# Tokens kept in natural order, values in chunks of 128 tokens, and a re-ordered start of the first batch

## The chip, the cores and the metric

The kernel runs on one core of one Trainium2 chip. The metric is the device time of one execution in microseconds (us). The median of three runs of the kernel before is 842.7 us (839.12 to 846.02).

## What is computed

Three blocks follow one another. All numbers are float32.

```python
# q, k, v: (4 batches, 8 heads, 576 tokens, 64);  M = 32 landmarks of 18 neighbouring tokens each
q_lm = q.reshape(B, H, 32, 18, D).mean(axis=3);  k_lm likewise
A  = softmax(q    @ k_lm.T / 8)      # 576 x 32
Bm = softmax(q_lm @ k_lm.T / 8)      # 32 x 32
C  = softmax(q_lm @ k.T / 8)         # 32 x 576
Z  = Bm.T / (norm_1(Bm) * norm_inf(Bm) + 1e-6)
for _ in range(6): Z = 2 * Z - Z @ Bm @ Z
x = (A @ Z @ C @ v)                  # heads side by side: 2304 tokens x 512
x = silu(x @ w_in) @ w_out           # first MLP: 512 -> 2048 -> 512
xn = x / rms(x) * rms_g              # second MLP: 512 -> 1536 -> 512
out = (silu(xn @ w_gate) * (xn @ w_val)) @ w_out2
```

## The kernel before

**Stages.** A head (0 to about 34 us) does the attention of batch 0 for both groups `g` of four heads, in an order written out by hand in the strings of `HEAD`. Each name there is a step (`qs00` is step `qs0` of group 0, `sc11` is `sc1` of group 1), and `go` records the steps one after the other. `Queue` makes every step's instructions follow the last one on the same engine, so the string is the order on each engine. Then the first MLP runs over batches 0 to 3, two halves of 288 tokens each (`moe1_h`, then `moe1_out`, LAG 3 steps later). The attention of the next batch is woven into it by the generators `attention` (g = 0, 1), whose order among the other work a scheduler sets by its own estimate of when operands are ready. From about 408 us the second MLP runs in 36 equal steps (`moe2_step`) on three blocks of 768 tokens.

**The attention's result is not formed.** The factor Z C v is multiplied into `w_in` first: `lt` holds minus (Z C v), `wprime` multiplies it with a quarter `nb_` of `w_in` into `W'` (`pw` in PSUM), and splits W' into a high and a low float32r part (`wp`: an ACT cast, then a DVE subtraction). `moe1_h` multiplies W' with the split softmax of A (`at`). So the first matmul `h` of a batch needs `lt`, `wp` and `at`.

**Token order.** The host lays q and k out as [64 x 2 partitions, 2, R = 18, M = 32]: the tokens of one landmark are 32 words apart. A sum over a landmark's 18 tokens is stored as row R of the same tile; in the head `summed` does it in one strided DVE reduction, or in five POOL additions where `BY_POOL` says so (three of the eight sums), and `landmarks` in six DVE additions for batches 1 to 3. The exponentials of C are written to `ec` in [32, 18] order (a stride of 18 words), so that v can come as [96 partitions, 4 heads, 6 tokens x 64]; `ct` then takes six transposes and `pu` 24 small matmuls per group. Since all later stages keep the landmark order, `split_x` reorders tokens when it splits x, and `store_out` writes pairs of rows 18 rows apart.

**Weights.** `w_in`, `w_out` and others come as 8-byte numbers and are converted on the chip by two ACT instructions (steps `Wa`, `oa`, lines 182, 183) and two DVE instructions (`Wd`, `We`, `od`, `oe`, lines 187, 189). In batch 0 `LOAD_AT` and `CONV_AT` say after which of the first steps a tile is loaded and converted, `WP_AT` when a further quarter of W' is made. `z1`, `y12` are spare matmuls (`spares`) which write nothing that is used.

Of the kernel before, what the change touches and what calls it, by code (L numbers as in the profile page):

```python
# [45 lines left out]
BY_POOL = {("q", 0, 0): False, ("q", 0, 1): True, ("q", 1, 0): False, ("q", 1, 1): True, ("k", 0, 0): False, ("k", 0, 1): False, ("k", 1, 0): False, ("k", 1, 1): True}  # L46
HEAD = [
    """y12 tab qs00 qs10 ks10 ks00 sc10 qs11 qs01 sc00 ks01 ks11 mx10 sc01 mx20 nb00 T00 ec10 mxl0 nb10 mA00 bbx0 T10
    sc11 su00 ec20 rc10 rr10 mA10 wa00 bbs0 cta0 su10 bbT0 mx11 ctb0 z1 bbd0 mx21 p10 ccb0 cca0 nb01 mxl1 nb11 T01
    z2 ec11 pua0 cr0 rc00 ic10 rr00 ec21 ic20 pub0 rt00 mA01 bbx1 rtu0 cta1 wa10 su01 rc11 rr11 rc01 pe00 z1 bbs1  # L50
    bbT1 bbd1 cp00 cca1 ctb1 rr01 wd00 p11 ccb1 wd10 pua1 xA00 xA01 pub1 cr1 xA10 ic11 pe10 sA01 z1 wa01 ic21 rtu1
    rt01 cp10 sA00 wa11 pe01 z1 wd01 pe20 z1 ms00 we00 cp01 oa13 pe11 cp20 z1 wd11 pe30 z1 we10 cp11 oa12 pe21 z1
    cp30 we01 pe40 z1 we11 cp21 pe31 z1 cp40 ms01 mr00 mr01 cp31 mu00 T11 pe50 pe41 mA11 z1 mu01 cp50 sb00 cp41 su11
    pe51 sb01 ac00 od12 pl0 cp51 ac01 pl1 al00 lt0 xA11 al01 lt1 sA10 tab2 pw z3 ms10 oe12 mr10 sA11 wc00 mu10 wc01
    ms11 wl00 wc10 wl01 wc11 wl10 oa14 wl11 sb10 od13""",
    """ac10 mr11 oe13 Wa00 mu11 al10 sb11""",
    """od14 ac11""",
    """al11 oa15 oe14 Wd00""",
    """od15 Wa10 We00 oe15 Wa11 Wd10""",
    """Wd11 Wa01 We10 We11""",  # L60
    """Wd01 We01""",
# [22 lines left out]
def nystrom_moe_kernel(ctx: ExitStack, tc: tile.TileContext, q, k, v, w_in, w_out, w_gate, w_val, w_out2, rms_g, out):  # L84
# [85 lines left out]

    def to_f32(c, raw, act=1024, dve=1024, out=None):
# [51 lines left out]
    def load_win(n, g):  # L223
# [6 lines left out]
        win_t[g, quarter(n)] = t  # L230

# [39 lines left out]

# [20 lines left out]
    def head(g):  # L292
# [32 lines left out]
        for x, y in (("q", q), ("k", k)):  # L325
            src[x] = big(f"{x}T", [P, 2, R + 1, M])
            SP.dma_start(out=src[x][:, :, 0:R], in_=y[0, g])
        yield
        vn = xp.tile([96, 4, 6 * D], F32, tag="x", name=f"vn_{n}")
        SP.dma_start(out=vn, in_=v[0, g])  # L330

        def summed(x, i):
            t = src[x][:, int(i)]
            if BY_POOL[x, g, int(i)]:
                d = sm("lms", [P, 2, 4, M]).rearrange("p i r l -> p (i r) l")
                QG.tensor_tensor(d, t[:, 0:8], t[:, 8:16], op=ALU.add)
# [34 lines left out]
        def _():  # L371
            QV.tensor_reduce(u["mx"][:, 1:2], c[2][:, :NC2], axis=AX.X, op=ALU.max)
# [1142 lines left out]
```

## Time and profile before

| | |
|---|---|
| median of 3 runs | 842.7 us |
| the profiled execution | 841.08 us |
| its span in the trace | 839.2 us |
| PE busy | 821.5 us, 98% |
| DVE busy | 534.6 us, 64% |
| ACT busy | 448.1 us, 53% |
| POOL busy | 20.8 us, 2% |

The trace covers the span; 1.9 us of the execution lie around it. A busy PE is not PE at its peak: the busy time counts from a matmul's start to its modelled end. PE is TensorE's matmuls, DVE VectorE, ACT ScalarE, POOL GpSimd, SP the engine that issues most DMAs. What matters is where PE has no work and what it waits for there.

### The profile page before, as it was taken

The numbers are of one execution on the slowest core, as the hardware profiler recorded it, in microseconds if no ns is written. First come the engines' busy times: TensorE is split into PE (matmuls) and PEld (weight loads), VectorE is DVE, ScalarE is ACT, GpSimd is POOL, SyncE is SP. The second block draws the span as 40 slices with busy tenths as digits, with TensorE's granted clock in tenths as the row PEclk, the third lists the DMA queues.
The fourth block names the chain that finished last, engine by engine and source line by source line (L and its number), as shares of the span: only waits on it lengthen the run. The fifth ranks groups of instructions, "written<-read, shape, count | busy, mean of one in ns | idle before, by whom it ended". The sixth has DMA issues, their size and how long they took to land.

```text
span 839.2 us, 15513 instructions
## 1 busy us (share of the span) xinstructions
PE 821.5 (98%) x5956; PEld 735.3 (88%) x5956; DVE 534.6 (64%) x1196; ACT 448.1 (53%) x927; POOL 20.8 (2%) x60
## 2 busy tenths in 40 slices
PE   7999999999999999999999999999999999999997
PEld 5667677988888989999999999999999999999996
DVE  6989868785679767769735389643558533333323
ACT  4886755775657767675734457433345323233222
POOL 5100000000000000000000000000000000000001
PEclk9999999999999999999999999999999999999999
DMA  9989557358886579988975458668565558655542
GB/s 304 393 286 326 196 170 258 121 176 299 285 289 193 167 263 354 351 304 295 329 309 189 174 197 286 242 228 295 210 226 209 183 184 289 226 222 189 181 197 76
DMA packets 72426, 202.87 MB, mean 242 GB/s; under 512 B 6592, under 2 KB 34240, under 8 KB 68384
## 3 DMA queue, kind: packets, MB, share of 16 engines
q1 hardware_dynamic: 72032, 201.09, 67.3%
q8 instruction: 47, 0.77, 0.4%
q0 software_dynamic: 240, 0.66, 0.3%
q14 instruction: 27, 0.22, 0.1%
q10 hardware_dynamic: 80, 0.13, 0.0%
HBM read 149.29 MB, written 52.56 MB: 241 GB/s over the span
## 4 chain that ended last, share of the span: by engine, by line
PE 87%; ACT 5%; DVE 4%; DMA 2%; issue 1%; POOL 1%; SPq 0%; POOLq 0%; ACTq 0%; DVEq 0%
PE ga L1180 18%; PE o L1254 18%; PE a L1031 18%; PE h L1011 10%; PE gc L1180 9%; PE gb L1180 5%; PE a L1028 3%; PE pw L843 2%; PE pe L270 1%; DMA r_g<-in_moe_w_gate_dram 1%; DMA qT<-in_q_dram 1%; PE pu L781 0%; PE pq L264 0%; POOL lms L284 0%; DVE hl L165 0%
## 5 line engine op out<-in xcount | busy, mean ns | idle before, releaser
L1031 PE MATMUL a<-hl,wo 128*128 128x288 f32 x1296 | 195.7, 299 | 2.2 <-ACT ex L1059 1.2
L1031 PEld LDWEIGHTS a<-hl,wo 128*128 128x128 f32 x1296 | 177.9, 188 | 8.5 <-issue 2.5
L1254 PE MATMUL o<-oc,u 128*128 128x512 f32 x648 | 178.9, 394 | 0.0
L1180 PE MATMUL ga<-x,w 128*128 128x384 f32 x840 | 171.1, 338 | 0.0
L1180 PEld LDWEIGHTS ga<-x,w 128*128 128x128 f32 x840 | 151.3, 188 | 12.4 <-ACT a L198 0.3
L1254 PEld LDWEIGHTS o<-oc,u 128*128 128x128 f32 x648 | 119.4, 188 | 13.6 <-DVE u L165 0.3
L1011 PE MATMUL h<-at,wp 128*128 128x288 f32 x768 | 129.3, 303 | 1.6 <-ACT wp L846 1.4
L1011 PEld LDWEIGHTS h<-at,wp 128*128 128x128 f32 x768 | 109.6, 188 | 18.2 <-issue 5.0
L198 DVE TENSOR_TENSOR v<-u,gc 128x384 f32<-128x384 f32 x72 | 39.8, 552 | 122.1 <-PE gc L1180 121.6
L1018 ACT ACTIVATE s<-h 128x288 f32<-128x288 f32 x108 | 44.1, 412 | 77.1 <-PE h L1011 75.3
L1180 PE MATMUL gc<-x,w 128*128 128x384 f32 x420 | 84.8, 336 | 0.0
L1180 PEld LDWEIGHTS gc<-x,w 128*128 128x128 f32 x420 | 75.0, 188 | 2.9
L198 ACT COPY u<-ga 128x384 f32<-128x384 f32 x72 | 34.5, 479 | 72.1 <-PE ga L1180 71.8
L198 DVE TENSOR_TENSOR u<-z,v 128x384 f32<-128x384 f32 x72 | 40.1, 557 | 46.7 <-ACT z L198 45.8
L164 ACT CAST u<-u 128x384 fp32r<-128x384 f32 x72 | 37.0, 513 | 61.4 <-DVE u L198 61.0
L165 DVE TENSOR_TENSOR hl<-s,hl 128x288 fp32r<-128x288 f32 x108 | 49.0, 453 | 20.4 <-ACT hl L164 19.7
L165 DVE TENSOR_TENSOR u<-u,u 128x384 fp32r<-128x384 f32 x72 | 40.1, 556 | 26.2 <-ACT u L164 25.9
L198 ACT ACTIVATE z<-ga 128x384 f32<-128x384 f32 x36 | 17.7, 492 | 68.5 <-PE ga L1180 68.3
L164 ACT CAST hl<-s 128x288 fp32r<-128x288 f32 x108 | 46.6, 433 | 2.7
L1028 PE MATMUL a<-s,wor 128*128 128x288 f32 x160 | 43.3, 409 | 0.0
L1180 PE MATMUL gb<-x,w 128*128 128x384 f32 x210 | 42.4, 336 | 0.0
L1180 PEld LDWEIGHTS gb<-x,w 128*128 128x128 f32 x210 | 37.0, 188 | 0.2
(230 smaller groups left out, 950.5 us busy)
## 6 DMA issues: line engine op xcount, KB each, us to landing
w<-w7d SPq DMA_DIRECT2D x31, 1792.0 KB, 7.4
oc<-wod SPq DMA_DIRECT2D x32, 512.0 KB, 7.8
win<-wind SPq DMA_DIRECT2D x20, 512.0 KB, 4.8
w2d<-c SPq DMA_DIRECT2D x36, 256.0 KB, 3.3
fw<-w2d SPq DMA_DIRECT2D x12, 768.0 KB, 6.4
winr<-in_moe_w_in_dram SPq DMA_DIRECT2D x8, 1024.0 KB, 10.2
wor<-in_moe_w_out_dram SPq DMA_DIRECT2D x16, 512.0 KB, 11.2
w7d<-w7p SPq DMA_DIRECT2D x16, 512.0 KB, 5.2
```

The lines of the kernel that those rows point to most:

```text
L164: x = ACT.copy(dst[:, 0], src) if hi is ACT else hi.tensor_copy(dst[:, 0], src)
L165: return x, lo.tensor_tensor(dst[:, 1], src, dst[:, 0].bitcast(F32), op=ALU.subtract)
L198: self.last = getattr(self.eng, name)(*args, **kw)
L270: eng.matmul(out[o], x[o], y[o], **kw)
L843: x = PE.matmul(pw[g][32 * i:32 * i + 32], lts[b][hr, i], win_t[i // 2, nb_][hr, i % 2], start=True, stop=True)
L1011: h_mm[0] = PE.matmul(ph, w[:, x, fo:fo + P], a[:, y, tk], start=i == 0, stop=i == 5)
L1018: ACT.activation(s, ph, AF.Silu)
L1028: PE.matmul(acc[d], w[:, y], hl, start=start, stop=stop)
L1031: PE.matmul(acc[d], w[:, x, y], hl[:, z], start=start and i == 0, stop=stop and i == 2)
L1180: mm[0] = PE.matmul(acc, w7[:, x, o, kk], xs[:, y, kk], start=start and n == 0, stop=stop and n == 5, skip_group_check=True)
L1254: PE.matmul(oacc[n], hls[j][:, x, t * P:(t + 1) * P], w[:, y], start=f == 0 and i == 0, stop=f == NF2 - 1 and i == 2)
```

## The change

Tokens keep their natural order everywhere: q and k are laid out as [128, 2, 576], the sums stand behind them in columns S to S + M, `ec` is [128, 576] and written contiguously. v comes as four chunks of 128 tokens and one of 64, in two DMAs per group (`values`); a group then takes five transposes (`turn`) and 20 small matmuls (`weigh`). `landmarks` is one DVE reduction per tensor, only one of the head's eight sums is still on POOL. `split_x` and `store_out` need no reordering. The first W' is made in three parts (`pwa`, `pwb`, `pwc`: 128, 128 and 256 columns) and the spare matmuls `z` are 128x128 with `ident` instead of 128x512 with `mean_w`. The strings of `HEAD` and the tables `WP_AT`, `LOAD_AT`, `CONV_AT` are new, and later quarters of W' in batch 0 have a raised priority for their matmuls and an explicit predecessor.

```diff
-BY_POOL = {("q", 0, 0): False, ("q", 0, 1): True, ("q", 1, 0): False, ("q", 1, 1): True, ("k", 0, 0): False, ("k", 0, 1): False, ("k", 1, 0): False, ("k", 1, 1): True}
+BY_POOL = {("q", 0, 0): False, ("q", 0, 1): False, ("q", 1, 0): False, ("q", 1, 1): True, ("k", 0, 0): False, ("k", 0, 1): False, ("k", 1, 0): False, ("k", 1, 1): False}
...
-    pe51 sb01 ac00 od12 pl0 cp51 ac01 pl1 al00 lt0 xA11 al01 lt1 sA10 tab2 pw z3 ms10 oe12 mr10 sA11 wc00 mu10 wc01
-    ms11 wl00 wc10 wl01 wc11 wl10 oa14 wl11 sb10 od13""",
+    T10 lt0 lt1 al01 Wa10 T11 pwa pwb mA11 pwc z1 mA10 wca0 su11 wca1 wla0 wcb0 wla1 wcb1 su10 wlb0 wcc0 wlb1 wcc1
+    wlc0 xA11 wlc1 xA10 sA11 tab2 ms11 sA10 mr11 ms10 od12 mu11""",
...
-WP_AT = (7, 9, 12)
+WP_AT = (7, 10, 14)
...
+    def values(b, g):
+        t = xp.tile([P, 5, 4, D], F32, tag="x", name=f"vn_{b}_{g}")
+        n = P * 16 * D
+        SP.dma_start(out=t[:, 0:4].rearrange("p c h d -> p (c h d)"), in_=v[b, g, 0:n].rearrange("(p f) -> p f", p=P))
+        SP.dma_start(out=t[0:VC[4], 4].rearrange("p h d -> p (h d)"), in_=v[b, g, n:].rearrange("(p f) -> p f", p=VC[4]))
+        return t
...
-                QV.tensor_reduce(t[:, R], t[:, 0:R].rearrange("p r l -> p l r"), axis=AX.X, op=ALU.add)
+                QV.tensor_reduce(t[:, S:], r, axis=AX.X, op=ALU.add)
...
-            QA.activation(keys()[:, R1:], c[2][:, :NC2].rearrange("p (r l) -> p r l", l=M), AF.Exp, ...)
+            QA.activation(keys()[:, C1:], c[2][:, :C2], AF.Exp, ...)
...
+        for x, lo, hi in (("a", 0, 128), ("b", 128, 256), ("c", 256, 512)):
+            y = slice(lo, hi)
+            step["pw" + x] = lambda y=y: mm(y)
...
-                VE.tensor_tensor(d, t[:, :, 0:4], t[:, :, 4:8], op=ALU.add)
-            for x in (8, 12):
-                VE.tensor_tensor(d, d, t[:, :, x:x + 4], op=ALU.add)
-            VE.tensor_tensor(d[:, :, 0:2], d[:, :, 0:2], d[:, :, 2:4], op=ALU.add)
-            VE.tensor_tensor(d[:, :, 0:2], d[:, :, 0:2], t[:, :, 16:R], op=ALU.add)
-            VE.tensor_tensor(t[:, :, R], d[:, :, 0], d[:, :, 1], op=ALU.add)
+                VE.tensor_reduce(t[:, :, S:], t[:, :, 0:S].rearrange("p i (l r) -> p i l r", r=R), axis=AX.X, op=ALU.add)
...
-            ACT.copy(blocked(t[:, 0, i]), by_landmark(c[:, i]))
+            ACT.copy(t[:, 0, i], c[:, i])
...
-            (SP, POOL, ACT)[h and last].dma_start(out=out[b * S:(b + 1) * S, :].rearrange("(l r) d -> l r d", r=R)[:, r:r + 2], in_=e[64 * h:64 * h + 64])
+            (SP, POOL, ACT)[h and last].dma_start(out=out[row + 64 * h:row + 64 * h + 64], in_=e[y])
```

The first place is DVE in the head, where the second group's chain of six iterations is set up. `cr_1`, `ic_1`, `rc_1` and `rt_0_125` belong to group 1, `pe_..` are the iterations of Z, `winr_0` and `win_0` the conversion of the first `w_in` quarter. Before:

```order
L284 COPY rt_1_124<-pe_0_0_352 128x96
L284 RECIPROCAL rc_1_233<-rc_1_233 128x1
L284 SCALAR_TENSOR_TENSOR winr_0_135<-winr_0_135 128x512 x2
L284 TENSOR_REDUCE cr_1_408<-p_0_1_373 128x2
L284 TENSOR_SCALAR ic_1_409<-cr_1_408 128x1
L284 TENSOR_REDUCE ms_1_232<-sa_1_228 128x9
L284 RECIPROCAL ic_1_409<-ic_1_409 128x1
L284 TENSOR_SCALAR rt_0_125<-pu_1_381,rc_1_233,ic_1_409 128x64
L284 SCALAR_TENSOR_TENSOR rt_0_125<-p_0_1_373,ic_1_409,id_98 128x32
```

and now:

```order
L309 TENSOR_REDUCE cr_1_364<-p_0_1_344 128x2
L309 TENSOR_SCALAR ic_1_365<-cr_1_364 128x1
L309 COPY rt_1_124<-pe_0_0_354 128x96
L309 RECIPROCAL ic_1_365<-ic_1_365 128x1
L309 TENSOR_REDUCE ms_1_227<-sa_1_223 128x9
L309 SCALAR_TENSOR_TENSOR rt_0_125<-p_0_1_344,ic_1_365,id_98 128x32
L309 TENSOR_SCALAR rt_0_125<-pu_1_370,rc_1_228,ic_1_365 128x64
L309 SCALAR_TENSOR_TENSOR winr_0_135<-winr_0_135 128x512
```

The weight conversion stood ahead of group 1's `rt`; now it stands behind it.

The second place is PE in batch 0, where the second quarter of W' is made (`pw_0`, eight rows in both, of which the last stands here) and first used (`h_0_0`). `a_..` are the products with `w_out`, named by half, part and output block. Before:

```order
L843 MATMUL pw_0_1_805<-win_1_155,lt_572 32x512
L1028 MATMUL a_1_0_0_788<-s_1_13_732,wor_147 128x288
L1011 MATMUL h_0_0_818<-at_0_552,wp_0_803 128x288 x2
L1028 MATMUL a_1_0_1_789<-s_1_13_732,wor_147 128x288
L1028 MATMUL a_1_0_2_790<-s_1_13_732,wor_147 128x288
L1011 MATMUL h_0_0_818<-at_0_552,wp_0_803 128x288
```

and now:

```order
L849 MATMUL pw_0_1_797<-win_1_160,lt_550 32x512
L1034 MATMUL a_0_0_0_690<-s_0_15_687,wor_153 128x288
L1034 MATMUL a_0_0_1_691<-s_0_15_687,wor_153 128x288
L1034 MATMUL a_0_0_2_692<-s_0_15_687,wor_153 128x288
L1034 MATMUL a_0_0_3_693<-s_0_15_687,wor_153 128x288
L1034 MATMUL a_1_0_0_780<-s_1_12_707,wor_147 128x288
L1034 MATMUL a_1_0_1_781<-s_1_12_707,wor_147 128x288
L1034 MATMUL a_1_0_2_782<-s_1_12_707,wor_147 128x288
L1034 MATMUL a_1_0_3_783<-s_1_12_707,wor_147 128x288
L1017 MATMUL h_0_0_810<-at_0_529,wp_0_795 128x288 x3
```

One `a` row stood between the last `pw_0` and the first `h_0_0`; now there are eight.

The third place is DVE at the same time: the low part of that quarter (`wp_0`) and the landmark sum of batch 1 (`qT_0` under L200). Before:

```order
L187 SCALAR_TENSOR_TENSOR wor_623<-wor_623 128x512
L189 SCALAR_TENSOR_TENSOR wor_623<-wos_798,wor_623 128x512
L187 SCALAR_TENSOR_TENSOR winr_2_619<-winr_2_619 128x1024
L847 TENSOR_TENSOR wp_0_803<-pw_0_0_804,wp_0_803 128x512
L847 TENSOR_TENSOR wp_0_803<-pw_0_1_805,wp_0_803 128x512
L189 SCALAR_TENSOR_TENSOR win_2_742<-win_2_742,winr_2_619 128x1024
```

and now:

```order
L309 SCALAR_TENSOR_TENSOR wor_153<-wos_710,wor_153 128x512
L200 TENSOR_REDUCE qT_0_819<-qT_0_819 128x2x32
L189 SCALAR_TENSOR_TENSOR winr_2_615<-winr_2_615 128x1024
L853 TENSOR_TENSOR wp_0_795<-pw_0_0_796,wp_0_795 128x512
L853 TENSOR_TENSOR wp_0_795<-pw_0_1_797,wp_0_795 128x512
```

The sum over q of batch 1, which needs a load, has come ahead of the low part of W'.

## Rows read from the trace of the kernel before

**Rows 1.** The page, part 1: engine, busy us (share of span), instructions.

```profile
PE 821.5 (98%) x5956; PEld 735.3 (88%) x5956; DVE 534.6 (64%) x1196; ACT 448.1 (53%) x927; POOL 20.8 (2%) x60
```

**Rows 2.** By stretch: length; busy PE, PEld, DVE, ACT, POOL; clock; DMA share, GB/s.

```profile
0.00:33.83 33.83, 27.35 (x444) 17.45 (x444) 25.89 (x77) 18.91 (x48) 14.54 (x48) 1.00 0.95 347
33.83:60.00 26.17, 24.81 (x151) 18.81 (x151) 22.18 (x35) 23.39 (x45) 0.99 (x1) 1.00 0.85 308
60.00:280.00 220.00, 215.92 (x2051) 183.20 (x2051) 173.70 (x452) 149.57 (x315) 2.41 (x6) 1.00 0.67 228
...
420.00:820.00 400.00, 399.78 (x2076) 371.12 (x2075) 199.25 (x384) 157.74 (x311) 0.00 (x0) 1.00 0.60 222
```

**Rows 3.** Order of time, PE, head: start, length, instruction, [idle before <-releaser].

```profile
13.82 0.43 PE L284 MATMUL pq<-qT,kT 64*32 64x288 f32 x1 [0.99 <-POOL kT L284]
...
22.96 0.37 PE L284 MATMUL pe<-rt 32*32 32x96 f32 x8 [0.32 <-DVE rt L284]
...
23.79 0.37 PE L284 MATMUL pe<-rt 32*32 32x96 f32 x8
...
33.83 3.49 PE L1011 MATMUL h<-at,wp 128*128 128x288 f32 x24
```

**Rows 4.** Order of time, DVE, head.

```profile
10.43 1.12 DVE L284 TENSOR_REDUCE kT<-kT 128x32 f32<-128x576 f32 x1 [0.30 <-DMA kT<-in_k_dram]
```

**Rows 5.** Order of time, POOL, head.

```profile
13.52 0.25 POOL L284 TENSOR_TENSOR kT<-lms 128x32 f32<-128x32 f32 x1
```

**Rows 6.** Groups by line and form: busy us, mean ns, idle before.

```profile
L284 DVE TENSOR_REDUCE kT<-kT 128x32 f32<-128x576 f32 x3 | 3.3, 1126 | 0.6 <-DMA kT<-in_k_dram 0.6
L198 DVE TENSOR_REDUCE ms<-sa 128x18 f32<-128x576 f32 x12 | 8.9, 739 | 0.3
L284 ACT ACTIVATE win<-winr 128x512 f32<-128x512 f32 x8 | 5.5, 692 | 0.0
L284 ACT ACTIVATE ec<-c,nb 128x320 f32<-128x320 f32 x2 | 1.7, 859 | 8.6 <-DVE nb L284 8.6
L284 ACT ACTIVATE sa<-sa 128x288 f32<-128x288 f32 x4 | 1.5, 436 | 0.0
```

**Rows 7.** The chain that ended last: start, length, what.

```profile
20.18 1.24 DVE winr L284 x2
...
98.07 0.81 PE pu L781 x48
...
107.29 0.67 PE ct L768 x6
```

**Rows 8.** Order of time, ACT, end of the head.

```profile
31.14 0.43 ACT L284 ACTIVATE sa<-sa 128x288 f32<-128x288 f32 x1
31.59 0.27 ACT L284 ACTIVATE lt<-pl 64x128 f32<-64x128 f32 x1
31.88 1.28 ACT L284 ACT_TABLE_LOAD   x1
...
33.41 0.65 ACT L284 CAST wp<-pw 128x256 fp32r<-128x256 f32 x2
```

**Rows 9.** Order of time, PE, its two longest gaps in batch 0.

```profile
53.40 0.54 PE L1011 MATMUL h<-at,wp 128*128 128x288 f32 x2 [1.36 <-ACT wp L846]
...
56.69 2.10 PE L1028 MATMUL a<-s,wor 128*128 128x288 f32 x8
...
104.33 2.30 PE L1031 MATMUL a<-hl,wo 128*128 128x288 f32 x15 [0.94 <-DVE e L1056]
```

**Rows 10.** DMA moved from 12 to 15 us, then from 18 to 21 us.

```profile
DMA packets 135, 0.72 MB, mean 240 GB/s; under 512 B 16, under 2 KB 16, under 8 KB 135
...
DMA packets 325, 1.22 MB, mean 408 GB/s; under 512 B 29, under 2 KB 29, under 8 KB 324
```

**Rows 11.** Order of time, SP's DMA queue.

```profile
51.48 0.64 SPq L672 DMA_DIRECT2D qT<-in_q_dram  x1
```

**Rows 12.** Spare matmuls of the start: ns min/median/max, first and last start.

```profile
L284 PEld LDWEIGHTS spare<-ident x24: 192/333/338, 1.5 to 5.8; 128*128 128x128 f32 x24
```

More of the change, by code (lines that the diff above doesn't have):

```diff
@@ L270, in blocks, with turn, weigh @@
             eng.matmul(out[o], x[o], y[o], **kw)
+    VC = (P, P, P, P, S - 4 * P)
+    def values(b, g):
[4 more added lines that the diff above has]
+        return t
+    def turn(tp, ec, c0, c1, eng=PE):
+        for c in range(c0, c1):
+            eng.transpose(tp[0:VC[c], c - c0], ec[:, c * P:c * P + VC[c]], ident)
+    def weigh(pu, ct, vn, c0, c1, eng=PE):
+        for c in range(c0, c1):
+            for h in range(4):
+                y = slice(32 * h, 32 * h + 32)
+                eng.matmul(pu[y], ct[0:VC[c], c, y], vn[0:VC[c], c, h ^ 1], start=c == 0, stop=c == 4)
     class Queue:
@@ L467, in _ @@
                 u["pu"] = ps(f"pu_{n}", [P, D])
-            for i in range(i0, i1):
-                for h in range(4):
-                    QP.matmul(u["pu"][32 * h:32 * h + 32], u["ct"][:, i, 32 * h:32 * h + 32], vn[:, h ^ 1, i * D:(i + 1) * D], start=i == 0, stop=i == 5)
+            weigh(u["pu"], u["ct"], vn, i0, i1, QP)
         @add("rc0")
@@ L617, in head_wprime, with mm @@
         pw = []
-        def mm():
-            pw.extend(ps(f"pw_0_{nb_}_{g}") for g in range(NG))
+        def mm(y):
+            if not pw:
+                pw.extend(ps(f"pw_0_{nb_}_{g}") for g in range(NG))
             for i in range(4):
@@ L638, in table, with spares @@
         step[name] = f
-    def spares(n, early):
-        if early not in spare:
-            spare[early] = pa.tile([P, 4, P], F32, tag="a", name=f"spare_{early:d}")
+    def spares(n, key):
+        if key not in spare:
+            spare[key] = pa.tile([P, P], F32, tag="a", name=f"spare_{key}")
         for _ in range(n):
-            if early:
-                QP.matmul(spare[early][:, 0], ident, ident, start=True, stop=True)
-            else:
-                QP.matmul(spare[early], mean_w, mean_w.unsqueeze(1).to_broadcast([P, 4, P]), start=True, stop=True)
+            QP.matmul(spare[key], ident, ident, start=True, stop=True)
     def attention(ap, b, g):
@@ L696, in attention @@
         yield
-        vn = load_v()
+        vn = values(b, g)
         yield
@@ L778, in attention @@
         with tc.high_priority(offset=PU_PRIO):
-            for i in range(6):
-                for h in range(4):
-                    PE.matmul(pu[32 * h:32 * h + 32], ct[:, i, 32 * h:32 * h + 32], vn[:, h ^ 1, i * D:(i + 1) * D], start=i == 0, stop=i == 5)
+            weigh(pu, ct, vn, 0, 5)
         VE.tensor_scalar(rc[:, 0:1], su[:, 0:1], su[:, 1:2], 1e-9, op0=ALU.add, op1=ALU.add)
@@ L835, in wprime @@
         pw = [ps(f"pw_{b}_{nb_}_{g}") for g in range(NG)]
-        x = None
-        for i in reversed(range(4)):
+        x = []
+        if b == 0:
+            x = [h_mm[0], *(win_ins["W{0}{1}0"] + win_ins["W{0}{1}1"] if nb_ == 0 else [win_ins[g, nb_] for g in range(NG)])]
+        for i in range(4):
             for g in range(NG):
```

170 lines of the change are left out of this document (79 added, 91 removed).

## The prediction

> **What bounds the kernel now.** I read first the busy shares, then the busy times by stretch, then PE's own order of time where it had gaps, and last the chain that ended last, for what released it there.
>
> PE is busy 821.5 of 839.2 us [rows 1], so at most 17.7 us can be won without taking work from it. The stretches show where these lie [rows 2]: 6.5 us in the head up to 33.83, 1.4 us up to 60, 4.1 us between 60 and 280, and 0.2 us in the 400 us of the second MLP. What the change does to `split_x` and to the stores therefore lies beside a full PE; I cost it at nothing. The last stores end the span, but they move the same rows of 2 KB, and I cost their new place at nothing too.
>
> In the head the length of a chain counts, not PE's work. Its stations are in PE's order of time [rows 3]: the last block of scores at 13.82, the second group's iteration (the one that `HEAD` calls pe01) at 22.96, the first `h` at 33.83. Between 22.96 and 33.83 PE runs at a fixed pace: iteration, spare, iteration in 0.83 us.
>
> **The change part by part.**
>
> *Sums in the head.* The last scores wait for POOL, whose last addition of the last sum starts at 13.52 and lasts 0.25 [rows 5]; they start at 13.82. DVE begins the sums of that k when it has landed, at 10.43 [rows 4]. Now DVE makes both. A strided sum takes 1.126 us, a contiguous reduction of the same 576 elements 0.739 [rows 6]. Two at 0.739 end at 11.9, and the scores can start at 12.05: 1.75 us earlier. If contiguous reading brought nothing, it would be two at 1.126, and 1.0 us earlier. I take 1.75, since the new access is that of the 0.739 row.
>
> *DVE's order.* On the chain stands a pair of weight conversions, 1.24 us from 20.18 on [rows 7], ahead of the second group's `cr`, `ic` and `rt`. The new order has it behind. So the two together give 3.0 us at most at pe01; at least 1.0, if DVE then lacks time elsewhere. I laid DVE's new order out with the durations of before, from the last sum to group 1's second `rt`: the queue is never empty for long, and pe01 starts at 20.2, so 2.75 us earlier. I take that.
>
> *Exponentials of C.* 320 columns, written with a stride, take 0.859; a contiguous exponential of 288 takes 0.436 [rows 6]. ACT wins some 0.4 on each of four. In the layout above DVE ends later than ACT at each of these places, so this gives nothing on the path; without that cover it would be 0.8 for the second group.
>
> *End of the head.* The second `lt` came behind an exponential (31.14 to 31.59 on ACT) and ended at 31.86; then a table load, the first cast of W' at 33.41 [rows 8] and `h` at 33.83, 1.97 after `lt`. Now the exponential and the load stand behind the casts, but two weight conversions ahead of them, at 0.692 each [rows 6] or less where they overlap, and the first cast has half the columns. That makes 1.4 to 1.8 after `lt`: 0.2 to 0.6 us, I take 0.4. The exponential is worth 0.45 at most; I take 0.25, since casts of `at` still stand there. The head: 2.75 + 0.25 + 0.4 = 3.4 us shorter.
>
> *What comes next in batch 0.* The table load is late now where it was early: the first `a` needs the silu behind it. The casts are done about 1 us after `h` starts, then two exponentials (0.436 each), the load with its dummy (1.5, from 31.88 to 33.41 [rows 8]) and the silu: 3.7 us, while the four `h` ahead of that `a` take 3.49 [rows 3]. That costs 0.25. The second half's `h` need `at`, cast on ACT behind the second silu and a weight conversion; I take 0.6 for that. So +0.85; bounds 0 (the order has other rows to run) and 2.
>
> *Second quarter of W'.* PE stood still for 1.36 us at 53.40, waiting for a cast of `wp` [rows 9]. Before, one `a` row stood between the matmuls of that quarter and the first `h` that uses it, now eight. Eight take 2.10 there, twice over 3.4, and the casts with the subtractions some 2. I take the whole 1.36 as gone; bounds 0 and 1.36.
>
> *PE's own work.* A group's `pu` takes 0.81 for 48 records, its `ct` 0.67 for six [rows 7]. Now there are 40 and five: 0.135 and 0.112 less, 0.25 for each of six groups in batches 1 to 3, where PE is busy 215.9 of 220 us [rows 2]. That is 1.5; bounds 0 and 1.5. In the head it is hidden behind DVE.
>
> *Landmark sums in batches 1 to 3.* One reduction over 1152 elements in place of six additions: DVE gets work taken away (173.7 of 220 us busy [rows 2]). PE waited 0.94 us at 104.33 for a DVE row [rows 9]; I take half of it, 0.5; bounds 0 and 0.94.
>
> *v.* While the two v of the head moved, the queues carried 240 GB/s; from 18 to 21 us, with weights, 408 [rows 10]. At 408 both v take 2.9 us instead of 4.9, so all later weights land 2 us earlier. Nothing in the head waits for these, so it is worth nothing here; it is a margin for the second rival. The Trainium skill ("SBUF — State Buffer", Door 1: The DMA port swizzle) says that 64 partitions reach only half of the 16 ports, so 96 rows take as long as 128 of that length; by that the old v would run at three quarters of the full rate, about 306 GB/s as an estimate, and the margin would be 0.9 us. The trace has it slower than that. The sum is the same by both, and the new small piece of 64 partitions would use half the ports.
>
> *Sum.* -3.4 + 0.85 - 1.36 - 1.5 - 0.5 = -5.9 us. The profiled execution took 841.08 us with a span of 839.2, so it would take 835.2. The median of the three runs is 842.7, 1.6 above it; in proportion 836.8. I predict 837.
>
> **The rivals.**
>
> *The head's gain is given back in batch 0* (no more than 3 us left). ACT is already full there: 23.39 of 26.17 us [rows 2]. In its new order the third silu stands behind three pairs of weight conversions (six at 0.692) and two casts of `at`; my layout has it end just when the `a` that needs it comes. Were each of these a little later, PE would wait there and again for the conversions ahead of `pw_0`, some 3 us in all: 838.2 for the profile, about 840 on the median. For it: both engines full. Against it: the weights land earlier, and one weight conversion is already done ahead of the casts of W'.
>
> *DVE waits for a load* (slower). The sum over q of batch 1 now stands ahead of the low part of the second W' quarter. DVE is in order, so a late q holds `wp_0`, and PE then holds at the first `h_0_0`. Before, SP issued this q at 51.48 [rows 11]; now it stands ahead of the last three `w_in` loads. By the sizes in the code 15.7 MB are ordered up to and with it; at 408 GB/s and a start near 3 us it lands at 42. DVE comes to it at about 44, and PE needs `wp_0` such that q may land up to 45.5. Each us beyond costs a us; the gain is used up at 51.4, that is if q were issued no earlier than before. Landed at 55, it would be 844.7, or 846 on the median.
>
> *Much more goes* (faster by more than 1%). All 4.08 us of PE's idle time between 60 and 280 could go with DVE's lighter load, instead of 0.5: 831.6, or 833.2 on the median. Against it: some of it was waits for ACT and loads.
>
> *The clock falls.* Spare matmuls are shorter now. At the start of the trace PE's weight loads take 333 ns and later 192 [rows 12], half clock and full clock (1.2 and 2.4 GHz), before and after a stretch of back-to-back spares; afterwards the granted clock is 1.00 through the whole head [rows 2]. If the clock fell in the head and rose again under the first `h`, I estimate 4 us, from the 3.49 us that four `h` take at full clock: 841 on the median. The Trainium skill ("TensorE: Matmul & The Clock Gate", What's actually happening) says that the slow state is the default and activity lifts it; the spares at the start agree. The new spares stream two passes of 128 columns where the old had 512 at one, and the gaps get shorter, so I hold this unlikely.
>
> **How the numbers follow.** The forecast has 0.57 (835 to 839.5), the gain given back 0.22 (839 to 842), the much larger gain 0.12, the late load 0.05, the clock 0.04. The range 833 to 842 holds the forecast, all but the edge of the second, half of the larger gain and the clock: a little over 0.8. A measurement of this kernel can tell about 1%, 8.4 us, from no change. Faster by more than that needs the larger gain: 0.12 and a little of the forecast's edge, 0.14. Slower by more than that needs a load later still than in the second rival: 0.03. The rest, 0.83, is within 1%.
>
> **What would show it.** In the trace of the changed kernel: the last block of scores near 12, pe01 near 20.2, the first `h` near 30.4; the wait ahead of the first `a` under 0.5 and those up to `pw_0` under 1; no wait of PE for `wp_0`; `pu` 40 records in 0.68; the second MLP at the same pace. I am wrong if the head is shorter by less than 2 us, if PE has a gap of more than 2 us between 31 and 60, or if PE's idle time between 60 and 280 changes by more than 2 us.

## The result and the profile after

The changed kernel takes 853.58 us (median of 19 runs, 845.43 to 855.56), the kernel before 842.31 in the same series (19 runs). The ratio is 1.012 [1.0101, 1.014]: 1.2% slower, where 837 was predicted and only 3 in 100 were given to slower by more than 1%. The profiled execution took 853.99 us, 12.9 more than that of before.

The first line to look at is the granted clock: 0.981 as a mean over the span, 0.999 before. By stretch (length; busy PE, PEld, DVE, ACT, POOL; clock; DMA share, GB/s), first the changed kernel:

```profile
12.00:16.00 4.00, 1.70 (x21) 0.66 (x9) 3.10 (x14) 2.15 (x8) 1.07 (x2) 1.00 1.03 391
...
13.50:15.30 1.80, 0.00 (x0) 0.00 (x0) 1.72 (x9) 0.65 (x2) 0.42 (x2) 1.00 1.03 369
...
17.00:18.00 1.00, 1.00 (x14) 0.81 (x13) 0.00 (x0) 1.00 (x7) 0.00 (x0) 0.67 1.04 426
18.00:44.00 26.00, 25.31 (x367) 17.92 (x367) 14.72 (x47) 11.67 (x30) 4.44 (x6) 0.50 0.81 316
...
45.00:46.00 1.00, 1.00 (x10) 1.00 (x9) 0.97 (x4) 0.98 (x4) 0.00 (x0) 1.00 1.01 413
...
60.00:280.00 220.00, 214.46 (x1929) 177.52 (x1928) 168.99 (x376) 147.18 (x309) 2.00 (x5) 0.99 0.67 232
```

and the first of these stretches in the kernel before:

```profile
12.00:16.00 4.00, 2.91 (x38) 1.25 (x27) 3.63 (x15) 2.88 (x9) 3.12 (x8) 1.00 1.02 243
```

PE of the changed kernel works 1.70 us of the 4 from 12 to 16, before 2.91, and nothing at all from 13.50 to 15.30. At about 17.3 us the clock falls to half (from 2.4 to 1.2 GHz) and comes back at about 44.6. From 18 to 44 PE is busy 25.31 of 26 us, so a look at busy shares alone finds nothing wrong there. Two of the 19 runs have a clock of 0.993 and 0.994 where the other 17 have 0.979 to 0.985; they took 847.52 and 845.43 us, the others 851.65 and more. Before, the clock is 1.00 through the whole head [rows 2]. The v loads do run faster, 391 GB/s where 243 were.

In PE's order of time (start, length, instruction, idle before and what released it) the same head reads:

```profile
13.11 0.30 PE L309 MATMUL ct<-ident,ec 128*64 128x128 f32 x1 [0.34 <-ACT ec L309]
15.36 0.63 PE L309 MATMUL ct<-ident,ec 128*128 128x128 f32 x4 [1.95 <-DVE rc L309]
16.66 0.71 PE L309 MATMUL spare_z<-ident 128*128 128x128 f32 x4 [0.68 <-ACT ct L309]
...
27.33 0.54 PE L309 MATMUL pe<-rt 32*32 32x96 f32 x8
...
28.75 0.55 PE L309 MATMUL pe<-rt 32*32 32x96 f32 x8
...
43.51 3.93 PE L1017 MATMUL h<-at,wp 128*128 128x288 f32 x24
```

The scores end early, as forecast. Then the four transposes of the keys (`cta0`) wait 1.95 us, until 15.36. The row names `rc`, which only happens to end last: what they need is a PSUM bank, which the transpose T01 on DVE frees:

```profile
14.74 0.47 DVE L309 STREAM_TRANSPOSE sa<-pq 128x288 f32<-128x288 f32 x1
```

The run t01_early below shows that it is this transpose. Iteration and spare then follow each other every 1.41 us instead of 0.83, pe01 stands at 27.33 and the first `h` at 43.51, where 33.83 was before [rows 3].

A second loss stands between 60 and 120 us, in PE's waits there (us in total, times, longest):

```profile
PE a L1034 <- DVE wor L191: 5.3, 4, 2.1
```

and in the order of time of DVE and then PE, at one of the four:

```profile
101.27 1.31 DVE L200 TENSOR_REDUCE kT<-kT 128x64 f32<-128x1152 f32 x1
...
103.90 0.69 DVE L191 SCALAR_TENSOR_TENSOR wor<-wos,wor 128x512 int32<-128x512 int32 x1
```

```profile
104.64 2.83 PE L1034 MATMUL a<-s,wor 128*128 128x288 f32 x8 [2.08 <-DVE wor L191]
```

A `w_out` tile is converted just when its `a` needs it. Before, PE had no wait for `wor` in this stretch; its one wait for DVE there was 0.94 us, for `e` [rows 9]. These eight `a` take 2.83 where others take 2.21: behind the 2.08 us wait the clock fell once more, from about 106.1 to 109.5.

Four points of the four kernels that matter most, in their profiled executions (us):

| kernel | first `h` | first `a` on split weights | first `ga` of the second MLP | whole time |
|---|---|---|---|---|
| before | 33.83 | 104.33 | 414.6 | 841.08 |
| changed | 43.51 | 120.0 | 427.6 | 853.99 |
| fill_gap (below) | 34.45 | 109.5 | 416.0 | 842.39 |
| nat_old_order (below) | 33.00 | 103.5 | 409.3 | 835.12 |

From before to changed: 9.7 us lost up to the first `h`, 6.0 more up to the first `a` on split weights, and 2.8 won behind it.

### The profile page after: what moved, and what is told of

It reads as the page before. It is cut to its first block, busy times and chain, and to the rows that moved or that the text cites. A ratio compares the mean times of both kernels' runs of the same rounds, so it can differ in the third digit from the quotient of the medians.

```text
span 852.2 us, 15430 instructions
## 1 busy us (share of the span) xinstructions
PE 832.5 (98%) x5932; PEld 744.5 (87%) x5932; DVE 530.6 (62%) x1140; ACT 441.8 (52%) x929; POOL 18.0 (2%) x50
## 4 chain that ended last, share of the span: by engine, by line
PE 92%; DVE 3%; ACT 3%; DMA 1%; issue 1%; POOL 0%; POOLq 0%; SPq 0%; ACTq 0%; DVEq 0%
PE a L1037 20%; PE ga L1178 18%; PE o L1252 18%; PE h L1017 11%; PE gc L1178 9%; PE gb L1178 4%; PE a L1034 3%; PE pw L849 2%; PE pe L273 1%; PE spare_z L309 1%; PE pe L309 1%; DMA win<-wind 1%; PE spare_y L309 1%; PE pu L295 1%; PE pq L267 1%
## 5 line engine op out<-in xcount | busy, mean ns | idle before, releaser
L200 DVE TENSOR_TENSOR v<-u,gc 128x384 f32<-128x384 f32 x72 | 39.7, 552 | 122.5 <-PE gc L1178 121.9
L200 ACT COPY u<-ga 128x384 f32<-128x384 f32 x72 | 34.5, 480 | 72.7 <-PE ga L1178 72.4
L200 DVE TENSOR_TENSOR u<-z,v 128x384 f32<-128x384 f32 x72 | 40.1, 557 | 46.6 <-ACT z L200 45.5
L200 ACT ACTIVATE z<-ga 128x384 f32<-128x384 f32 x36 | 17.7, 492 | 68.9 <-PE ga L1178 68.6
L1034 PEld LDWEIGHTS a<-s,wor 128*128 128x128 f32 x160 | 29.1, 190 | 18.4 <-DVE wor L191 6.2
```

The costliest lines, as they stand in the source:

```text
L200: self.last = getattr(self.eng, name)(*args, **kw)
L1034: PE.matmul(acc[d], w[:, y], hl, start=start, stop=stop)
```

## Experiments

Theory A: the thin stretch from 12.7 to 16.7 us lets the clock fall, and the half clock behind it is most of the loss. Theory B: the new order of batch 0, above all the later conversions, costs by itself. Rivals: the new spares are too light for the clock (C); DVE and ACT are full in batch 0, so that any order costs the same (D); the amount of PE's work in the head counts, not its place (F). Ratios are against the kernel before, run beside each. The mean granted clock of the runs stands in the table because it differs between executions of one kernel, and the times with it. That holds for the kernel before too: its 80 runs beside these experiments have clocks of 0.987 to 1.000 and took 839.89 to 848.31 us, with a median of 840.4 at 0.999 and 1.000 (ten runs) and of 846.7 at 0.987 and 0.988 (five).

| kernel | median us (runs) | lowest to highest | clock of the runs | ratio |
|---|---|---|---|---|
| changed | 853.58 (19) | 845.43 to 855.56 | 0.979 to 0.994 | 1.012 |
| fill_gap | 844.03 (10) | 842.39 to 846.40 | 0.995 to 0.999 | 1.0019 [1.0002, 1.0036] |
| wide_spares | 852.86 (4) | 852.21 to 854.93 | 0.980 to 0.984 | 1.0123 [1.009, 1.0156] |
| before_narrow | 844.86 (10) | 840.89 to 845.94 | 0.990 to 0.999 | 1.0012 [0.9993, 1.0031] |
| t01_early | 842.34 (10) | 841.00 to 851.12 | 0.982 to 0.998 | 1.0021 [0.9985, 1.0057] |
| fill_late | 847.96 (10) | 844.62 to 850.77 | 0.992 to 0.999 | 1.0055 [1.0031, 1.008] |
| t01_fill | 843.45 (10) | 841.83 to 844.81 | 0.996 to 0.999 | 1.0009 [0.9995, 1.0024] |
| fill_conv | 840.09 (10) | 839.49 to 841.90 | 0.998 to 1.000 | 0.9974 [0.9956, 0.9993] |
| t01_fill_conv | 839.43 (12) | 838.15 to 841.09 | 0.998 to 1.000 | 0.9963 [0.9949, 0.9977] |
| nat_old_order | 837.47 (6) | 835.12 to 839.37 | 0.992 to 1.000 | 0.9945 [0.9923, 0.9966] |
| nat_late_conv | 839.72 (10) | 838.62 to 842.74 | 0.993 to 0.999 | 0.9960 [0.9939, 0.9981] |
| nat_fill | 836.13 (6) | 835.78 to 837.31 | 0.996 to 0.999 | 0.9924 [0.9901, 0.9948] |
| nat_fill_wp | 835.21 (5) | 834.77 to 836.97 | 0.998 to 1.000 | 0.9913 [0.9884, 0.9942] |

### The clock

**fill_gap**: more spares in the thin stretch. The code here and below shows only the part of a line that changes. `Y10` is ten spares of `ident` against 128 columns, in a PSUM tile of their own.

```diff
-nb10 T00 bbx0 sc11 mA00
+nb10 T00 bbx0 sc11 Y10 mA00
```

> The changed kernel with ten more spare matmuls (128x128, ident) on PE between the scores of group 1 and the transposes of the keys, where PE of the changed kernel did 1.70 us of work from 12 to 16 us; nothing else. Theory A (that thin stretch lets the clock fall to half at about 17 us, and the 27 us at half clock are what the kernel lost): granted clock 1.00 from 16 to 44 us, a pe step with its spare about every 0.85 us instead of 1.41, first h near 33 instead of 43.51, whole time 838 to 843. Rival B (the new order of batch 0 costs by itself, above all PE's 5.3 us of waits for DVE's wor conversions between 60 and 120 us): the head is as A says, but the waits for wor stay at 4 to 6 us and the time is 844 to 848. Rival C (the spares against ident are too light for the clock, wherever the gap is): the clock still falls, a few us later, and the time stays at 849 to 854.

The time fell by 9.55 us. By stretch:

```profile
12.00:16.00 4.00, 3.84 (x47) 3.05 (x33) 3.27 (x15) 2.36 (x8) 1.07 (x2) 1.00 1.03 376
16.00:20.00 4.00, 3.20 (x63) 2.26 (x60) 1.68 (x8) 3.54 (x12) 0.75 (x2) 1.00 1.03 418
20.00:24.00 4.00, 3.45 (x95) 2.61 (x99) 3.21 (x15) 3.35 (x7) 0.32 (x1) 1.00 1.02 418
```

The clock is 1.00 in every stretch of the head, an iteration with its spare takes 0.83 again, and the first `h` stands at 34.45. That takes C out as the cause: with the thin stretch filled, the clock stays up through the head though all other spares are the light ones. The waits for `wor` stayed at 5.3 us, as B said. The time, too, lies at the lower end of B's band and not in A's.

**wide_spares**: the changed kernel with the heavier spares of before (`mean_w` against 512 columns) at all places marked z.

> The changed kernel with the spares of the head (all but the first ones) as the kernel before has them: mean_w against 512 columns instead of ident against 128; nothing else. Theory A (the thin stretch ahead of them lets the clock fall): the first of these spares stands at 16.66 us, behind the thin stretch, so the clock falls at about 17 us as it did, and the time stays at 850 to 855. Rival C (the spares are too light): clock 1.00 from 16 to 44 us, first h near 33, 838 to 843.

```profile
12.00:16.00 4.00, 1.71 (x31) 0.73 (x20) 3.52 (x17) 2.45 (x8) 1.07 (x2) 1.00 1.05 384
16.00:20.00 4.00, 3.33 (x37) 1.96 (x39) 0.89 (x5) 3.43 (x11) 0.04 (x1) 0.68 1.02 417
20.00:24.00 4.00, 3.32 (x50) 2.18 (x43) 1.96 (x10) 1.49 (x4) 1.03 (x2) 0.50 1.02 416
```

852.86, as A said: same thin stretch, same fall at about 17.4, and back at about 41.3. The heavier spares neither kept the clock up nor brought it back soon.

**before_narrow**: the kernel before with the light spares.

> The kernel before with the spares of the head as the changed kernel has them: ident against 128 columns instead of mean_w against 512; nothing else. Theory A: its clock does not fall, since PE worked 2.91 us of 12 to 16, and the time is 842 within 1.5 us. Rival C: the clock falls to half in the head, first h near 44 instead of 33.83, 850 to 854.

The ratio is 1.0012 [0.9993, 1.0031], so C's large loss is not there. The median, 844.86, lies above A's 842 within 1.5, and A's sentence that the clock does not fall was too simple. In the profiled execution (845.60 us) it fell after all, at another place:

```profile
26.00:27.00 1.00, 1.00 (x19) 0.66 (x19) 1.00 (x3) 0.96 (x3) 0.00 (x0) 1.00 1.02 414
27.00:28.50 1.50, 0.06 (x1) 0.00 (x0) 0.45 (x1) 0.11 (x1) 0.00 (x0) 1.00 1.03 404
...
29.00:29.50 0.50, 0.50 (x17) 0.44 (x16) 0.00 (x0) 0.00 (x0) 0.00 (x0) 0.56 0.96 393
30.00:39.00 9.00, 9.00 (x96) 5.23 (x96) 6.25 (x19) 4.62 (x13) 2.60 (x4) 0.50 1.04 410
```

and in its list of PE's waits:

```profile
PE spare L284 <- issue: 1.6, 1, 1.6
```

PE stood still for 1.6 us, for nothing that the profile shows ("issue"), and soon after it, at about 29.1, the clock went to half for some 10 us; the first `h` came at 39.03. So a short stand is followed by a fall in the order of before too. What made PE stand there stays open.

**fill_late**: the same ten spares, behind the stretch.

```diff
-ctb0 cta0 z2 bbT0
+ctb0 cta0 z12 bbT0
```

> The changed kernel with the ten extra spares of fill_gap put behind the transposes of the keys (at 16.66 us) instead of ahead of them; nothing else: the same extra work on PE, but the thin stretch from 12.7 to 16.66 us stays as it was. Theory A (it is that stretch): the clock falls at about 17 us as in the changed kernel, in nearly all runs, and the time is 852 to 858 (the ten spares add 2 to 4 us to the head). Rival F (it is the sum of PE's work in the head that counts, wherever it stands): the clock holds, 842 to 846.

```profile
12.00:16.00 4.00, 1.71 (x29) 0.79 (x13) 3.35 (x15) 2.40 (x8) 1.07 (x2) 1.00 1.03 391
...
18.00:20.00 2.00, 2.00 (x11) 2.00 (x11) 0.00 (x0) 1.69 (x5) 0.00 (x0) 0.50 1.03 416
20.00:21.00 1.00, 1.00 (x8) 1.00 (x7) 0.00 (x0) 0.00 (x0) 0.00 (x0) 0.57 1.00 397
21.00:22.00 1.00, 1.00 (x16) 0.84 (x15) 0.00 (x0) 0.00 (x0) 0.00 (x0) 1.00 1.05 430
```

and in PE's order of time:

```profile
16.91 4.57 PE L309 MATMUL spare_z<-ident 128*128 128x128 f32 x24 [0.68 <-ACT ct L309]
```

In the profiled execution the clock fell at 17.5, as A said, which it did not in fill_gap's with the same ten spares in another place. So place counts, and F is not enough. But A's price missed: 847.96 instead of 852 to 858. The row of twelve spares ran from 16.91 to 21.5, and in it the clock came back, at about 20.9. So the loss has two parts: what lets the clock fall (the thin stretch), and how long it stays down, 3.4 us here and 27.3 in the changed kernel, with other work on PE behind the fall. And A's "in nearly all runs" was wrong too: four of the ten runs have a clock of 0.999 (844.62 to 845.88, inside F's band), the other six 0.992 to 0.995 (847.68 to 850.77). One program, then, and the fall comes in some executions. The profiled one, 847.68, also has a second fall, from about 99.4 on, behind a wait of 2.06 us for `wor` ahead of 99.07.

**t01_early**: the wait itself taken away.

```diff
-rr10 rc00 bbs0 ctb0 cta0
+rr10 rc00 T01 bbs0 ctb0 cta0
...
-mxl1 nb01 nb11 T01 ccb0
+mxl1 nb01 nb11 ccb0
```

> The changed kernel with one transpose on DVE (T01, group 1's query block out of its PSUM bank) moved from behind the maxima of group 1 (14.74 us) to ahead of them (about 13.3); nothing else. The transposes cta0 wait for that bank. Expected: cta0 at 13.9 to 14.3 instead of 15.36, PE's wait ahead of it 0.5 to 0.9 instead of 1.95, pu near 17.5. Theory A: PE does about 2.4 us of work from 12 to 16; if that is enough to hold the clock, first h near 32 and 836 to 841; if not, the clock falls about as before and the time is 851 to 854. Rival B: first h near 32, but the waits for wor stay, 843 to 847. Rival C: clock falls all the same, 850 to 854.

```profile
13.91 0.66 PE L309 MATMUL ct<-ident,ec 128*128 128x128 f32 x4 [0.34 <-DVE sa L309]
...
22.16 0.37 PE L309 MATMUL pe<-rt 32*32 32x96 f32 x8
...
32.55 3.73 PE L1017 MATMUL h<-at,wp 128*128 128x288 f32 x24
```

The bank was the cause of the wait: `cta0` now stands at 13.91 and waits 0.34. Seven of ten runs took 841.0 to 843.2 at a clock of 0.996 to 0.998, three took 850.3 to 851.1 at 0.982 to 0.984. So the clock fell in some executions and not in others, at some 9 us each. Where it held, the time lies between A's 836 to 841 and B's 843 to 847; the waits for `wor` stayed, at 5.2 us. PE works 2.65 of the 4 us from 12 to 16 now.

**t01_fill** (T01 early and five spares in the stretch):

> The changed kernel with T01 early (as t01_early) and five spares (128x128, ident) on PE between the scores of group 1 and the transposes of the keys. Theory A: where t01_early alone had its clock fall in 3 of 10 runs (850 to 851 against 841 to 843), the spares hold it in every run: all runs at 841 to 844, clock 0.995 or more, the first h near 32.8; the waits for wor stay at 5 us. Rival C (the clock's fall has nothing to do with the thin stretch): still some runs at 850.

All ten runs at 0.996 or more, 841.83 to 844.81, two of them above the band of 841 to 844: no run near 850 is left, and the waits for `wor` stay at 5.3 us, as expected.

### The conversions

**fill_conv** puts three tables of before into fill_gap:

```diff
-WP_AT = (7, 10, 14)
-LOAD_AT = {3: "o8", 4: "o9", 5: "o10", 6: "o11", 7: "n30", 8: "n31", 9: "o12", 10: "o13", 11: "o14", 12: "o15"}
-CONV_AT = {6: "n20", 7: "n21", 8: "o4", 9: "o5", 10: "n30", 11: "n31", 12: "o6", 13: "o7", 14: "o8", 15: "o9",
-           16: "o10", 17: "o11", 18: "o12", 19: "o13", 20: "o14", 21: "o15"}
+WP_AT = (7, 9, 12)
+LOAD_AT = {3: "n30", 4: "n31", 5: "o8", 6: "o9", 7: "o10", 8: "o11", 9: "o12", 10: "o13", 11: "o14", 12: "o15"}
+CONV_AT = {4: "n20", 5: "n21", 6: "o4", 7: "o5", 8: "n30", 9: "n31", 10: "o6", 11: "o7", 12: "o8", 13: "o9",
+           14: "o10", 15: "o11", 16: "o12", 17: "o13", 18: "o14", 19: "o15"}
```

> The changed kernel with the ten spares of fill_gap, and with three tables of batch 0 as the kernel before has them: when the later weights are loaded, converted and made into W' (LOAD_AT, CONV_AT, WP_AT); so the w_out tiles are converted two steps earlier each. Theory B (the later conversions are the second cost, 5.3 us of PE waits for wor): PE's waits for wor fall below 1.5 us in total and the time is 3.5 to 5 us under fill_gap's 844.0, at 839 to 840.5. Rival D (DVE and ACT are the bound of that stretch, and an earlier conversion only makes the next thing late): waits of another kind, for s or wp, take their place, and the time stays within 1.5 us of 844.

840.09, 3.9 us under fill_gap. PE's waits from 8 to 130 us:

```profile
PE a L1034 <- ACT s L309: 1.3, 1, 1.3
PE a L1037 <- DVE e L1062: 1.0, 1, 1.0
...
PE a L1034 <- DVE wor L309: 0.5, 1, 0.5
```

The 5.3 us for `wor` became 0.5, and PE waits 1.0 for `e`, about as before. B holds, D falls. Not all of the 3.9 us is the waits themselves: fill_gap's runs have clocks of 0.995 to 0.999, fill_conv's 0.998 to 1.000. The runs at 0.999 alone (842.39 and 842.76 against five from 839.49 to 840.07) lie 2.8 us apart.

**nat_late_conv** does the reverse: nat_old_order (next) with the three tables of the changed kernel.

> nat_old_order (natural order and v in chunks with the old order of the work, 837.5 us) with the three tables of batch 0 as the changed kernel has them (later weights converted two steps later); nothing else. Theory B: PE waits 3.5 to 5.5 us more for wor between 60 and 110 us and the time is 841 to 843. If the tables cost only beside the new head: 837 to 839.

839.72, 2.25 more than nat_old_order: between the two bands. The waits for `wor` are there,

```profile
PE a L1037 <- DVE wor L191: 4.5, 3, 2.1
...
PE h L1020 <- DVE wp L856: 0.8, 1, 0.8
```

but the wait for `wp` went from 1.60 to 0.77 and that for `e` is gone, 1.8 us back. Behind one of the waits for `wor` the clock fell here as well, from about 91.2 to 94.6, so eight `a` take 3.61:

```profile
91.73 3.61 PE L1037 MATMUL a<-s,wor 128*128 128x288 f32 x8 [2.06 <-DVE wor L191]
```

By medians the tables cost 2.3 us with the old head and 3.9 with the new one. Most of that difference goes with the clock: at 0.999 they cost 2.6 here (838.62 and 838.84 against 836.16) and 2.8 there. These are few runs.

### The layout alone

**nat_old_order**: the changed kernel's token order and chunks of v, with `BY_POOL`, `HEAD`, the three tables and the spares of before. The three parts of the first W' and the raised priority and explicit predecessor of the later quarters stay as in the changed kernel.

> The natural token order and v in chunks of 128 tokens alone: the changed kernel with BY_POOL, HEAD, LOAD_AT, CONV_AT, WP_AT and the spares of the kernel before (the three parts of the first W' one behind the other where the whole stood). By the sum of the prediction the layout by itself is worth 1.5 us for pu and ct in six groups, about 1 us in the head for v and the contiguous exponentials, and nothing elsewhere: 838.5 to 841.5, clock 0.995 or more, first h at 32.5 to 34. If the layout costs something by itself: over 843.5 with the clock up.

837.47, better than expected, ratio 0.9945; its profiled execution, the fastest of the six, took 835.12, where the prediction's sum for the changed kernel came to 835.2. By stretch:

```profile
60.00:104.00 44.00, 42.98 (x316) 32.17 (x315) 37.74 (x76) 31.29 (x66) 0.40 (x1) 1.00 0.67 250
104.00:130.00 26.00, 26.00 (x310) 20.51 (x310) 18.53 (x61) 15.45 (x35) 0.40 (x1) 1.00 0.58 192
130.00:280.00 150.00, 149.94 (x1450) 132.90 (x1450) 115.61 (x264) 103.31 (x223) 1.60 (x4) 1.00 0.69 228
```

and in its chain that ended last (start, length, what):

```profile
97.20 0.83 PE pu L295 x40
...
106.30 0.56 PE ct L288 x5
107.53 0.83 PE pu L295 x40
```

PE's idle time between 60 and 280 is 1.08 us (1.02, 0 and 0.06) where it was 4.08 [rows 2]. `ct` is 0.11 shorter than in [rows 7]; `pu` is not: 40 records take 0.83, 48 took 0.81. So the layout, with these small changes that stayed in, is good for 5.5 us by medians (842.94 less 837.47), and what came with it, the order, the tables, the sums moved to DVE and the spares, lost 16: 853.58 less 837.47.

### A version that beats both

**t01_fill_conv**: T01 early, five spares, tables of before.

> The changed kernel with all three: T01 early, five spares ahead of the transposes, and the three tables of batch 0 as before. Theories A and B together: clock 0.995 or more in every run, first h near 32.8, waits for wor below 1.5 us, 836 to 839, a ratio of 0.993 to 0.997. Rival D: 841 to 843.

839.43 [0.9949, 0.9977]: faster than both kernels, though just above the 836 to 839 that were expected, and slower than nat_old_order. Its profiled execution, 841.09 and the slowest of the twelve, lost 1.4 us in two waits for "issue" in the head.

**nat_fill**: nat_old_order with five spares where PE waits for POOL's sum (`T10 sc11` becomes `T10 Y5 sc11`).

> nat_old_order with five spares (128x128, ident) on PE in the idle stretch between the first and the second half of group 1's scores (11.8 to 13.45 us, where PE waited for a sum on POOL); nothing else. The spares end before that sum, so nothing is delayed. Theory A: the runs of nat_old_order at a clock of 0.992 to 0.997 (837 to 839.4) are gone: clock 0.998 or more, all runs at 835 to 837.5, median near 836. If those slower runs come from another place than the head: no change, 837.5 with the same spread.

```profile
12.00:16.00 4.00, 3.42 (x34) 2.28 (x32) 3.28 (x14) 2.88 (x10) 2.72 (x7) 1.00 1.04 377
```

PE works 3.42 us of that stretch. In nat_old_order it works 2.27, with gaps of 1.48 us (ahead of 10.84) and 1.39 (ahead of 13.45) and scores between them. The six runs took 835.78 to 837.31 at 0.996 to 0.999, one of them under the 0.998 that was expected; nat_old_order had two runs at 839.25 and 839.37, with clocks of 0.993 and 0.992. So part of the spread of that kernel seems to be the clock too; where it fell in those runs no trace shows, and the ratios of the two kernels overlap.

**nat_fill_wp**: also `WP_AT = (6, 9, 12)`.

> nat_fill with the second W' of batch 0 made one step earlier (WP_AT 6 in place of 7), which PE waited 1.60 us for at 52.79 us (h on ACT's casts of wp). Expected: that wait gone, 1.0 to 1.6 us less than nat_fill, 834 to 836; or, if ACT and DVE are full there, a wait for s or wor in its place and the same time as nat_fill.

835.21, inside the band of 834 to 836: the wait for `wp` is gone from the list. The medians are 0.9 us apart where 1.0 to 1.6 was expected, and the intervals of the two ratios overlap. Against the kernel before the ratio is 0.9913 [0.9884, 0.9942].

## Why the prediction was wrong

**The step that failed** is the rival "The clock falls". The prediction had the mechanism on its list, but gave it 0.04 and 4 us, and nothing in its sum. Both numbers rest on one sentence each. "The gaps get shorter, so I hold this unlikely" did not come true: PE's waits ahead of 17 us add up to 4.57 us (1.60, 0.34, 1.95, 0.68) where they were 4.61 (1.57, 1.59, 0.99, 0.46), and their place is another. With the scores 2.3 us earlier and the transposes not, 2.97 of them gathered in one stretch, 12.7 to 16.7 us. And the price assumed that the clock would rise again under the first `h`, which it did, but counted only that `h`: the 26 us of the head at half speed ahead of it were the price. fill_gap measures it at 9.55 us by medians. The two profiled executions are 11.6 us apart: 9.06 up to the first `h` (43.51 less 34.45), 1.4 more up to the first `a` on split weights, where the changed kernel's clock falls again, and the rest behind that, unplaced. The prediction's reading of the start of the trace, weight loads of 333 ns as half clock, is borne out: the changed kernel's loads of that shape take up to 333 ns at half clock and 186 at full, though the profile's clock column reads 1.00 over the first 6 us. Without the fall, at fill_gap's 844.03, the prediction would still have missed its range; the steps below say by what. The Trainium skill ("TensorE: Matmul & The Clock Gate", What's actually happening), which the prediction cited, says that the slow state is the default and activity lifts it. The runs agree on the fall and, in fill_late, on the rise; but PE was busy 25.31 of 26 us in the changed kernel from 18 to 44, mostly with 32x32 iterations and spares, and the clock stayed at half.

**Sums in the head: right in kind, and too small.** The last block of scores was expected at 12.05; it starts at 11.54, 2.28 us earlier than before instead of 1.75.

**DVE's order, pe01 at 20.2: wrong by 2 us even at full clock.** It stands at 27.33 in the changed kernel, 23.82 in fill_gap and 22.16 in t01_early. The hand-made layout of DVE's order left out the PSUM bank that `cta0` needs, which DVE frees only behind three maxima and two products; the 1.66 us between fill_gap and t01_early are mostly that. It also took DVE for the chain. In t01_early, where the bank comes in time, DVE waits for PE, and PE runs through its own rows with two waits, 0.67 us ahead of 15.25 and 0.68 ahead of 18.89, for ACT's copies of `ct`:

```profile
16.56 0.22 DVE L309 TENSOR_REDUCE cr<-p 128x2 f32<-128x64 f32 x1 [1.25 <-PE p L309]
```

Of the 2.75 us expected at pe01, 0.8 are there in t01_early and none in the changed kernel's own order.

**End of the head and what comes next.** At full clock (t01_early) the first `h` comes at 32.55, 1.28 earlier than before instead of 3.4. The cost behind it was taken as 0.85 and is 1.54: `a` waits 1.26 for the silu, `h` 0.28 for `at` (fill_gap to t01_fill show 1.3 and 0.3 alike).

**Second quarter of W': right.** In the changed kernel no wait for `wp` stands in PE's list.

**The rival "given back in batch 0" was right in its place, not in its rows.** Given 0.22, it was priced at 3 us from ACT's order at 33 to 60. What costs is in the tables: by `CONV_AT` every tile from n20 to o15 is converted two steps later than before, and 5.3 us of PE's time wait for `w_out` tiles between 60 and 120. The three tables were changed back together, so `CONV_AT` is not shown apart from `LOAD_AT` and `WP_AT`. The diff showed the two steps; the prediction never set the step of a conversion against the step whose `a` uses the tile. The tables cost 3.9 us by medians, some 2.8 at equal clock.

**PE's own work: half right.** `ct` is shorter by 0.11 per group as forecast, `pu` not at all: 40 records, 32 with 128 rows and 8 with 64, take 0.83 us (0.68 was forecast), 48 with 96 rows took 0.81. Of 1.5 us some 0.7 are there.

**Landmark sums: right in direction, too small, and in another place.** The wait for `e` at 104.33, of which half was to go, is 0.98 in nat_old_order, as before. But the small waits of batches 1 and 2, in the stretches where PE of before stood 1.11 and 2.00 us,

```profile
130.00:170.00 40.00, 38.89 (x392) 34.37 (x391) 33.44 (x89) 25.07 (x55) 0.40 (x1) 1.00 0.55 184
...
236.00:280.00 44.00, 42.00 (x399) 37.87 (x398) 37.75 (x106) 32.59 (x70) 0.80 (x2) 1.00 0.66 210
```

are gone in nat_old_order (none and 0.06 left) and in the changed kernel (0.08 and 0.06). They were not waits for DVE's sums in the main:

```profile
PE a L1031 <- ACT ex L1059: 1.2, 1, 1.2
PE pq L264 <- issue: 1.1, 2, 0.7
```

That is most of the rival "much more goes". Which of the layout's parts took them away (the sums on DVE, the contiguous exponentials on ACT) was not tried apart.

**v, q of batch 1, the second MLP: right.** v moves at 391 GB/s and helps nothing in the head; SP issues q at 39.44 and nobody waits for it; the second MLP keeps its pace.

That the sum of -5.9 us came out in nat_old_order (5.96 between the two profiled executions) is partly chance: the head gave 0.8 instead of 3.4, the idle time between 60 and 280 3.0 instead of 0.5, `ct` 0.7 where `pu` and `ct` were to give 1.5, and the wait for `wp`, which was to go, is 1.60. Some 1.5 us of the gain stay unplaced.

## What to carry to other kernels

Lay PE's idle time out by place, not by sum: a change that makes the start of a chain earlier can gather the gaps ahead of its next link, and where the clock falls there, PE is slower from then on (an iteration with its spare 1.41 us instead of 0.83 here) though it looks busy. When an order is moved by hand, follow for each moved instruction the PSUM bank it takes and who frees it, and for each table of steps subtract the step of the maker from that of the user. Ten spares in the longest gap won 9.55 us here, the same ten behind it 5.62. A layout and a new order are best measured apart.

## What the runs showed of the hardware

- The granted clock fell behind short stands of PE: 1.95 us ahead of 15.36 in the changed kernel (fall at 17.3), 1.6 ahead of 28.66 in before_narrow (29.1), 2.08 ahead of 104.64 in the changed kernel (106.1). It did not follow every such gap (none behind the 1.71 us ahead of 118.16 in the changed kernel), nor in every execution of one program: by their mean clock, 4 of 10 in fill_late and 7 of 10 in t01_early kept it through the head. The Trainium skill ("TensorE: Matmul & The Clock Gate", What's actually happening) says that the same kernel is seen with different counts of slow matmuls from run to run. It says so of the start of a kernel; these runs show the same of falls within one.
- A busy PE did not raise it again at once. It stayed at half for 27 us of the changed kernel's head, with light spares, and for 24 us in wide_spares, with heavy ones. It came back under the first `h` in the one (`h` starts at 43.51, the clock is back at 44.6), under `pl` in the other (40.48, 41.3), and inside a row of twelve 128x128 spares in fill_late (16.91, 20.9).
- The time of `pu`, small matmuls of 64 columns, did not go by records alone: 40 with 128 or 64 rows took 0.83 us, 48 with 96 rows 0.81.
- A DVE reduction of 1152 contiguous elements to 64 takes 1.31 to 1.35 us, in place of six additions.
- PE stood for 1.6 us in before_narrow with nothing to wait for in the profile (DVE worked 0.45 and ACT 0.11 of the 1.5 us from 27.0); where that comes from stays open.
